# Halved inverse constants, parameters transposed on TensorE, a matmul broadcast of the log step, a pre-scaled input and a new instruction order in a state-space mixing kernel

## The chip, the cores and the metric

The kernel runs on one core of one Trainium2 chip. The metric is the device time of one execution in microseconds (us). The profile's span, from the first to the last instruction, is 1.8 us shorter than the time of the same run. "Before" and "after" below are the kernels without and with the change. Some executions fall in a second, slower state; only those in the fast state are compared.

In the traces PE is TensorE (PEld its weight loads), DVE is VectorE, ACT ScalarE, POOL GpSimd and SP SyncE; "PE ps L743" is what line 743 of the kernel writes to PSUM, the memory that holds TensorE's results, and AR is the on-chip memory SBUF. To evict is to copy a result out of PSUM. A clock, where one is shown, is TensorE's as the throttle granted it, as a share of full speed.

## The reference, cut to what matters

```python
x = A_u                                              # 2048 x 512, bf16
g = sigmoid((x * gate_w).sum(-1, keepdims=True))     # one number per row
# branch a: state-space layer, as a long convolution per channel
dt = exp(log_dt);  logdA = dt * (A_re + 1j*A_im);  dB = dt * (B_re + 1j*B_im)
P = exp(logdA[:, :, None] * arange(2048))            # 512 x 128 x 2048
K = einsum("dn,dnl,dn->dl", C_re + 1j*C_im, P, dB).real
a = irfft(rfft(pad(x)) * rfft(pad(K)))[:2048] + x * Dskip
# branch b: the two rows of x with the highest x @ w_r go through a small gated
# network; their results are added to those two rows of x
b = x + scatter(...)
return g * a + (1 - g) * b
```

The kernel computes K from two tables (powers of a step, in two levels) whose product is a matmul. The Fourier transforms are matmuls with constant matrices: the forward constants ("c_fwd") and the inverse constants ("c_inv", 2 MB). The 512 channels go in two halves, called half 0 and half 1. Branch b's updated input is written to a copy in main memory ("xp", by a scatter of two rows) and reloaded.

## The kernel before

Every operation is put on record with what it reads, what it writes and an estimated cost. A list of numbers, SEQ, then fixes the order in which all of them go to their engines; where an operation may run on ScalarE or VectorE, a minus sign means VectorE. Each engine runs its share of the list strictly in order.

```python
for n in SEQ:                                   # the fixed order
    o = ops[n if n >= 0 else ~n]
    if o.alt is not None:
        o.eng = DVE if n < 0 else ACT           # minus: VectorE
```

Cuts are marked "..." in all code below. The head: the six parameter matrices come through transposing transfers, and the log step is spread over 128 partitions by its transfer.

```python
def prm_t(i):
    P.op(SP, lambda h: h.dma_start_transpose(PRM(0, 128, i * D, (1, D)), dr(prm[i], ...)), ...)
DQ([(LDT(0, 128, 0, (1, D)), dr(A_log_dt, 0, (0, 128), (1, D)))], [], [LDT], 131072, eng=ACT)
...
AC(f512(DTB), f512(LDT), ACTF.Exp, [LDT], [DTB], tset=0)
TT(f512(AL), f512(DTB), f512(PRM, 0), ALU.mult, ...)          # the first product
```

The second table of each half is completed by two complex products, six VectorE operations each:

```python
cmul(h, sl(13, 8), sl(0, 8), bn(1, 8), ...)     # four products, a subtraction, an addition: 2048 elements each
cmul(h, sl(9, 4),  sl(5, 4), bn(0, 4), ...)     # the same with 1024
```

The forward transform is eight jobs of matmuls, each into a pair of PSUM banks that ScalarE or VectorE then evicts; there are two such pairs (`pb = fwp[k % 2]`). The spectra are multiplied on VectorE; some products are summed by accumulating transfers that the GpSimd queue issues (`dma_start(..., accum_op=add)`). The inverse constants come as one 2 MB load, behind the complex products. In the inverse, 32 matmuls subtract the input, so that g * (y - x) + x gives the result:

```python
last = hh.matmul(pb(...), G(...), X(...), start=(q + e + c == 0), stop=False)
if q:
    last = hh.matmul(pb(...), CB(0, 128, 768, (1, 128)), U(...), start=False, ...)   # minus x
```

## Time and profile before

| | before |
|---|---|
| time, median of 4 runs | 184.59 us (182.49 to 187.02) |
| profiled run, its span | 182.6 us, 180.8 us |
| VectorE busy, idle | 153.9, 26.9 us |
| first product of VectorE starts | 6.68 us |
| last product ends, last result computed, span ends | 170.0, 176.0, 180.8 us |

Those four runs spread by 4.5 us. In the five later sets of runs, of seven each, this kernel's median was 182.6 to 183.2 us. Here are lines of the DMA table (columns: output and input, issuing queue, count, size of one, median us from issue to landing):

```profile
AR<-AR POOLq DMA_DIRECT2D x8, 512.0 KB, 5.6
AR<-c_inv SPq DMA_DIRECT2D x1, 2048.0 KB, 11.5
AR<-xp SPq DMA_DIRECT2D x2, 1024.0 KB, 12.1
```

The first line is the accumulations. The second and third transfers, 4 MB together, are issued at 122.24 and 129.55 us, among those accumulations.

### The profile page before, as it was taken

The numbers are of one execution on the slowest core, as the hardware profiler recorded it, in microseconds if no ns is written. First come the engines' busy times: TensorE is split into PE (matmuls) and PEld (weight loads), VectorE is DVE, ScalarE is ACT, GpSimd is POOL, SyncE is SP. The second block draws the span as 40 slices with busy tenths as digits, with TensorE's granted clock in tenths as the row PEclk, the third lists the DMA queues.
The fourth block names the chain that finished last, engine by engine and source line by source line (L and its number), as shares of the span: only waits on it lengthen the run. The fifth ranks groups of instructions, "written<-read, shape, count | busy, mean of one in ns | idle before, by whom it ended". The sixth has DMA issues, their size and how long they took to land.

```text
span 180.8 us, 3701 instructions
## 1 busy us (share of the span) xinstructions
PE 137.5 (76%) x1550; PEld 92.1 (51%) x1558; DVE 153.9 (85%) x240; ACT 118.6 (66%) x207; POOL 18.7 (10%) x26
## 2 busy tenths in 40 slices
PE   0039797996988999759946773689739999999970
PEld 0014263432555443444614552686528788888860
DVE  0377999899999998997879999989948999999570
ACT  2599999989999799999985272163501584425100
POOL 3000000000000000001000000053100125350500
PEclk9999996999996999987997999569987999999997
DMA  5999999595703950001621000079999659979995
GB/s 56 280 325 230 284 283 381 242 450 154 266 4 99 373 170 0 4 4 15 261 67 52 0 0 5 2 141 268 305 224 356 182 100 187 163 82 186 152 186 155
DMA packets 28338, 30.25 MB, mean 167 GB/s; under 512 B 13431, under 2 KB 22914, under 8 KB 28162
## 3 DMA queue, kind: packets, MB, share of 16 engines
q1 hardware_dynamic: 22626, 23.88, 42.6%
q0 software_dynamic: 4352, 5.77, 20.1%
q10 hardware_dynamic: 1344, 0.36, 1.8%
q8 instruction: 12, 0.20, 0.4%
q14 instruction: 4, 0.03, 0.1%
HBM read 19.26 MB, written 4.20 MB: 130 GB/s over the span
## 4 chain that ended last, share of the span: by engine, by line
ACT 33%; DVE 27%; PE 24%; DMA 10%; issue 3%; DVEq 0%; ACTq 0%
DVE AR L401 26%; ACT AR L413 14%; PE ps L892 10%; DMA AR<-AR 6%; ACT AR L587 6%; PE ps L743 5%; ACT AR L417 4%; PE ps L758 4%; DMA AR<-in_A_A_re_dram 3%; ACT AR L421 3%; ACT AR L583 2%; PE ps L761 2%; PE ps L895 1%; ACT L413 1%; PE ps L805 1%
## 5 line engine op out<-in xcount | busy, mean ns | idle before, releaser
L401 DVE TENSOR_TENSOR AR<-AR 128x1024 bf16<-128x1024 bf16 (+8 forms) x135 | 120.3, 931 | 13.8 <-DMA AR<-in_A_A_re_dram 6.7
L417 ACT ACTIVATE AR<-ps 128x1024 bf16<-128x1024 f32 (+3 forms) x41 | 34.2, 856 | 31.3 <-PE ps L827 20.1
L413 ACT ACTIVATE AR<-AR 128x256 bf16<-128x256 f32 (+5 forms) x91 | 40.4, 516 | 2.9 <-DVE AR L401 1.9
L743 PE MATMUL ps<-AR 128*128 128x512 bf16 x124 | 31.7, 410 | 13.2 <-DMA AR<-in_A_u_dram 11.8
L892 PE MATMUL ps<-AR 128*128 128x256 bf16 x256 | 33.9, 279 | 3.7 <-DMA AR<-c_inv 3.3
L892 PEld LDWEIGHTS ps<-AR 128*128 128x128 bf16 x256 | 25.3, 100 | 8.1 <-DVE AR L401 4.5
L743 PEld LDWEIGHTS ps<-AR 128*128 128x128 bf16 x128 | 13.1, 105 | 29.2 <-DMA AR<-in_A_u_dram 11.8
L827 PE MATMUL ps<-AR 128*128 128x256 bf16 x160 | 21.1, 291 | 6.9 <-ACT AR L417 6.9
L827 PEld LDWEIGHTS ps<-AR 128*128 128x128 bf16 x160 | 16.3, 105 | 11.5 <-ACT AR L417 8.6
L427 POOL DMA_DIRECT2D AR<-AR x14 | 14.8, 1194 | 68.0 <-DVE AR L401 56.9
L758 PE MATMUL ps<-AR 128*128 128x512 bf16 x60 | 16.3, 412 | 3.3 <-DVE AR L417 1.3
L791 PE MATMUL ps<-AR 128*64 128x42 bf16 x512 | 11.6, 203 | 7.4 <-DVE AR L401 4.6
L413 ACT ACTIVATE AR<-ps,AR 128x256 bf16<-128x256 f32 x24 | 10.1, 473 | 10.1 <-PE ps L895 7.7
L791 PEld LDWEIGHTS ps<-AR 128*64 128x64 bf16 x512 | 11.0, 132 | 9.2 <-DVE AR L401 4.9
L587 ACT ACTIVATE AR<-AR 128x1024 bf16<-128x1024 int16 (+1 forms) x14 | 14.5, 1052 | 0.6 <-DVE AR L401 0.3
L421 DVE TENSOR_SCALAR AR<-AR 128x256 int32<-128x256 f32 (+2 forms) x42 | 12.3, 333 | 0.9 <-ACT AR L587 0.9
L758 PEld LDWEIGHTS ps<-AR 128*128 128x128 bf16 x64 | 6.4, 105 | 10.5 <-issue 2.2
L417 DVE CAST AR<-ps 128x1024 bf16<-128x1024 f32 (+2 forms) x9 | 8.7, 979 | 1.7 <-PE ps L805 0.7
L945 POOL MEMSET AR<- 128x256 bf16 x2 | 0.7, 390 | 82.2 <-PE ps L791 82.2
L895 PE MATMUL ps<-AR 128*128 128x256 bf16 x32 | 8.7, 273 | 0.0
L421 ACT ACTIVATE AR<-AR 128x256 int32<-128x256 f32 x22 | 7.9, 407 | 0.2
L583 DVE TENSOR_SCALAR AR<-AR 128x1024 int32<-128x1024 int32 (+1 forms) x9 | 6.1, 673 | 2.1 <-ACT AR L413 2.1
(50 smaller groups left out, 85.6 us busy)
## 6 DMA issues: line engine op xcount, KB each, us to landing
AR<-AR POOLq DMA_DIRECT2D x8, 512.0 KB, 5.6
AR<-c_ksp SPq DMA_DIRECT2D x5, 512.0 KB, 3.9
AR<-c_fwd SPq DMA_DIRECT2D x4, 512.0 KB, 5.8
AR<-in_A_u_dram SPq DMA_DIRECT2D x2, 1024.0 KB, 8.1
AR<-c_inv SPq DMA_DIRECT2D x1, 2048.0 KB, 11.5
AR<-xp SPq DMA_DIRECT2D x2, 1024.0 KB, 12.1
out_dram<-AR SPq DMA_DIRECT2D x16, 128.0 KB, 3.4
AR<-in_B_w_up_dram SPq DMA_DIRECT2D x2, 896.0 KB, 8.4
```

The lines of the kernel that those rows point to most:

```text
L401: return P.op(DVE, lambda h: h.tensor_tensor(out=o, in0=a, in1=b, op=op), rd, wr, cost=tt_cost(o, a, b), **k)
L413: return P.op(ACT, lambda h: h.activation(out=o, in_=a, func=func, scale=scale, bias=bias), rd, wr, cost=0.185 + nel(o) * 0.833e-3 + (0.09 ...
L417: return P.op((ACT, DVE), (lambda h: h.activation(out=o, in_=a, func=ACTF.Copy), lambda h: h.tensor_copy(o, a)), rd, wr, cost=(0.185 + n * ...
L421: return P.op((ACT, DVE), (lambda h: h.activation(out=o, in_=a, func=ACTF.Copy, scale=c), lambda h: h.tensor_scalar(out=o, in0=a, scalar1= ...
L427: P.op(POOL, lambda h: h.dma_start(o, i, accum_op=ALU.add), rd, wr, cost=1.4, nbytes=nbytes, dma=True, tag="sum")
L587: return x.activation(out=so(2), in_=lo, func=ACTF.Sin, scale=-SC16 if m else SC16, bias=HPI(0, 128, 0, (1, 1)) if m else 0.0)
L743: last = h.matmul(o, F[ft](0, 128, ((par * 4 + st) * 2 + part) * 128, (1, 128)), U(0, 128, (blk * 8 + st * 2 + par) * D, (1, D)), start=(i ...
L758: last = h.matmul(o, F[ft](0, 128, ((4 + st) * 2 + part) * 128, (1, 128)), UN(0, 128, st * D, (1, D)), start=False, stop=(st == 3 and blk ...
L791: last = hh.matmul(pb(64 * ct, 64, (g - b0) * 42, (1, 42)), TP[h][1 - part](0, 128, g * 128 + ct, (2, 64)), TQ[h][1 - part](0, 128, g * 84 ...
L827: last = hh.matmul(pb(0, 128, n * 256, (1, 256)), KPU[u](0, 128, tau * 128, (1, 128)), KC[h](0, 128, jg * 256, (1, 256)), start=(k == 0), ...
L892: last = hh.matmul(pb(0, 128, e * 256, (1, 256)), G(0, 128, ((par * 2 + part) * 4 + ft) * 512 + (2 * t2 + e) * 128, (1, 128)), X(0, 128, h ...
L895: last = hh.matmul(pb(0, 128, e * 256, (1, HC)), CB(0, 128, 768, (1, 128)), U(0, 128, (blk * 8 + (2 * t2 + e) * 2 + par) * D + h * HC, (1, ...
```

## The change

The intent is to take the known waits away and to relieve the engine that is busiest. The core of the diff, part by part, with most arguments cut:

```diff
 # 1 the head: plain loads, transposes on TensorE, a 1 KB log step spread by a matmul
-    P.op(SP, lambda h: h.dma_start_transpose(PRM(...), dr(prm[i], 0, (128, D), (1, 128))), ...)
+    DQ([(PRM(0, 128, i * D, (1, D)), dr(prm[i], 0, (D, 128), (1, D)))], [], [(PRM, i)], 131072)
+P.op(PE, lambda h: h.matmul(LP(...), ONE(0, 1, 0, (1, 128)), LDT(0, 1, 0, (1, D)), ...), ...)
+AC(f512(DTB), f512(LP), ACTF.Exp, [LP.buf], [DTB], tset=0)
+    ... last = h.transpose(pt(...), PRM(...), CB(0, 128, 0, (1, 128)))           # 24 of them
+TT(w512(AL), w512(DTB), t512(PT0), ALU.mult, [DTB, (PT0.buf, 0)], [AL])
 # 2 half 0's second table: four products, no add and no subtract; TensorE sums them
+    TT(sl(1, j, c), sl(1, s, c), bv(br), MUL, ...);  TT(sl(0, j, c), sl(0, s, c), bv(br), MUL, ...)
+    TT(xv(1), sl(0, s, c), bv(nb), MUL, ...);        TT(xv(0), sl(1, s, c), bv(bi), MUL, ...)
+    if h == 0:
+        last = hh.matmul(pb(...), TP[h][1 - part](...), EX[h][1 - part](...24 columns...), start=False, ...)
 # 3 a third PSUM pair in the forward transform (and two more banks for the table product)
-    pb = fwp[k % 2]
+    pb = (*fwp, fw2)[k % 3]
 # 4 inverse constants: two buffers of 1 MB, each with a home of its own, loaded apart
-DMA([(G(0, 128, 0, (1024, 8), (1, 1024)), dr(g_c, ...))], [], [G], 2097152)
+ld_g(0)      # right after half 1's second table in program order
+ld_g(1)      # after half 0's complex products
 # 5 the reload earlier; the input scaled by 1 - g there, and no subtraction in the inverse
+for tb in range(16):
+    P.op((ACT, DVE), (... h.activation(out=o, in_=o, func=ACTF.Copy, scale=SG(0, 128, 48 + tb, (1, 1))) ...))
-    last = hh.matmul(pb(...), CB(0, 128, 768, (1, 128)), U(...), start=False, ...)
 # 6 a new SEQ of 645 operations for 620; half of the last outputs leave on ScalarE's queue
```

## The prediction

> **What bounds the kernel now.** I read the page first (busy times, slices, chain), then the waits, then the timeline of VectorE, ScalarE and the DMA issues, and last a table by stage. The page:
>
> ```profile
> PE 137.5 (76%) x1550; PEld 92.1 (51%) x1558; DVE 153.9 (85%) x240; ACT 118.6 (66%) x207; POOL 18.7 (10%) x26
> ...
> DVE  0377999899999998997879999989948999999570
> ACT  2599999989999799999985272163501584425100
> ...
> DMA  5999999595703950001621000079999659979995
> ...
> ACT 33%; DVE 27%; PE 24%; DMA 10%; issue 3%; DVEq 0%; ACTq 0%
> ```
>
> VectorE is busy for 153.9 of 180.8 us. ScalarE is just as full in the first half (slices 2 to 21) and half idle after it. So there are two regimes: until about 95 us both engines are saturated and hand work to each other; after that VectorE alone sets the pace, and PE takes over at the very end. A gain must either take work from VectorE or close its 26.9 us of idle. The table by stage (stretch, length, then busy us and count of PE, PEld, DVE, ACT, POOL, then clock, DMA share, GB/s) says where that idle is:
>
> ```profile
> 0.00:6.68 6.68, 0.00 (x0) 0.00 (x0) 0.00 (x1) 1.91 (x2) 1.72 (x9) 1.00 0.72 101
> 6.68:15.00 8.32, 3.18 (x8) 1.19 (x9) 5.42 (x15) 7.57 (x19) 0.00 (x0) 1.00 1.07 315
> 15.00:80.00 65.00, 56.60 (x630) 29.41 (x633) 62.85 (x113) 62.65 (x115) 0.00 (x0) 0.95 0.64 200
> 80.00:100.00 20.00, 14.91 (x159) 8.61 (x163) 16.89 (x28) 16.85 (x22) 0.71 (x2) 0.84 0.28 89
> 100.00:127.00 27.00, 19.03 (x378) 15.43 (x376) 25.83 (x31) 11.16 (x19) 4.22 (x4) 0.87 0.32 78
> 127.00:140.00 13.00, 9.10 (x67) 7.32 (x68) 9.88 (x12) 3.33 (x4) 0.85 (x1) 0.87 1.02 288
> 140.00:154.20 14.20, 13.76 (x124) 11.65 (x122) 14.03 (x18) 8.40 (x14) 4.97 (x6) 1.00 0.74 159
> 154.20:175.10 20.90, 20.90 (x190) 18.50 (x190) 18.14 (x27) 6.71 (x16) 6.22 (x5) 1.00 1.03 156
> 175.10:180.80 5.70, 0.01 (x1) 0.00 (x0) 0.88 (x2) 0.00 (x0) 0.00 (x0) 0.82 0.49 142
> ```
>
> Idle of VectorE by row: 6.7 head, 2.9, 2.2, 3.1, 1.2, 3.1 (127 to 140), 0.2, 2.8, 4.8 tail. Two rows have a named cause in the waits:
>
> ```profile
> DVE AR L401 <- DMA AR<-in_A_A_re_dram: 6.7, 1, 6.7
> ...
> PE ps L892 <- DMA AR<-c_inv: 3.3, 1, 3.3
> ...
> DVE AR L401 <- DMA AR<-AR: 3.0, 2, 2.5
> ```
>
> The head is the parameter that comes through a transposing DMA. At 127 to 140 us VectorE waits for an accumulating DMA of its products while the 2 MB of inverse constants (issued at 122.24) and the 2 MB reload of the input (issued at 129.55) share the DMA engines; the chain of waits holds one such accumulation for 11.73 us, against a median of 5.6 us in the table of DMA issues. At the end PE runs without a gap from 154.2 to 175.1 us and VectorE waits for it.
>
> **What the skill says.** "VectorE: DVE Perf Modes", section "The perf-mode tier table", has a bf16 two-tensor operation of 2048 elements at 1224 ns, and at one element per cycle with fp32 or PSUM operands. The trace agrees: 1219 ns for 128x2048 bf16, and 1217 ns for 128x1024 with fp32 output. So parameters read from PSUM cost nothing extra where the output is fp32 anyway. "ScalarE: Activation LUTs", section "What ACT_TABLE_LOAD costs", has 186 ns plus 0.833 ns per element for one ACTIVATE, some 93 ns for a per-partition scale, and 93 ns of overlap back to back; the trace has 618 ns for 128x512, as it would have it. "DMA: Bandwidth & Descriptors", section "Issuing engines are not separate DMA queues", says that transfers of all issuers share the same 16 engines; the stretched accumulation above agrees. "TensorE: Matmul & The Clock Gate", section "Part 4: PE-mode transpose", says that such a transpose writes PSUM and took about 275 ns in one kernel; this trace has only four fp32 ones, of 300 ns.
>
> **Part by part.**
>
> *Head.* Six transposing DMAs go, each holding the issuing queue 1.2 to 2.1 us and landing after 5 to 8 us. Plain 128 KB loads take their place; the plain 128 KB load of the log step landed in 4.1 us. The log step itself shrinks to 1 KB (other 1 KB loads: about 5 us with three issues ahead of them; as first on its queue I estimate 3.5 to 4). Then come one small matmul (0.3), the exponential after its table load, which ends at 4.1 (0.6), and the first product (0.7). I put VectorE's first product at 5.2 us instead of 6.68, and ScalarE's exponentials at 5.9 instead of 7.40: 1.5 us. ScalarE then does 35 exponentials in a row at 313 ns (5.01 us for 16 now), to about 17 us; VectorE meanwhile has angles, the C-times-B products and the first evictions, some 12 us, so most of the 2.9 us of idle in the second row goes too. The added eviction of the transposed B costs VectorE 0.7 to 1.2 us.
>
> *VectorE work.* In the second table of half 0 the two complex products lose their add and subtract: two operations of 2048 at 1219 and two of 1024 at 687 ns, 3.8 us less; a negation of 512 comes in (0.3). The order list marks operations that VectorE takes with a minus. Counting them: 8 evictions of 1024 instead of 5 (3 x 1.22 = 3.7 more), 35 angle scalings of 256 instead of 32 (0.9 more), one 512 cast less (0.7), fewer 504 casts (0.3), fewer copies in the routing (four or so at 0.17, 0.7). With the B eviction at 1.2: -3.8 + 0.3 + 3.7 + 0.9 + 1.2 - 0.7 - 0.3 - 0.7 = +0.6 us. So VectorE's total does not fall; the saved work pays for evictions taken off ScalarE.
>
> *ScalarE work.* 3 evictions less (3.0), 3 scalings less (1.2), exponentials of the second table in halves: 18 x 0.40 instead of 9 x 0.62 (+1.7), a sixteen-part scaling of the reloaded input of which 15 are here (15 x 0.62 = 9.3). The last item is in the second regime, where ScalarE is half idle. In the first regime it loses about 2.5 us. Table loads stay at six by the order list.
>
> *PE.* Added: 256 matmuls of 24 columns for half 0; 512 of the same line take 11.6 us now, so at most 5.8 us, beside work of the saturated engines, and 24 transposes in the head. Removed: the 32 matmuls that subtract the input in the inverse (their slots in the chain are 0.11 us each), of which some 21 are in the gapless stretch at the end: 21 x 0.11 = 2.3 us.
>
> *DMA.* The inverse constants come as two loads of 1 MB, the first while the second half's tables are being multiplied; the reload comes before the products. Near the accumulations only 1 MB is left. I expect them near 5.6 us, with five products of 1.22 us to cover them: the 3.1 us wait falls to 0.5 or so.
>
> *The end.* With 2.3 us less of PE work and earlier constants, PE has no backlog. After the last product there remain 32 matmuls (3.5 us) and one pair of results, against about 5.6 us from the last product (170.0) to the end of the results: 1.5 to 2 us. Half of the second half's outputs go out on ScalarE's queue: 0.4 us at most (one issue).
>
> *Sum.* Head 1.5, gap after it 1.5, saturated stage 1.5 (ScalarE sheds 2.5, VectorE gains 1.3 there), accumulation 2.5, end 1.8, small items 0.3, less 0.6 for VectorE's total: 8.5 us. From the other side: 5.2 head + 154.5 busy + idle of 4 (saturated stage), 1.2, 0.7, 0.4, then 3.9 and 4.0 after the last product makes 173.9 against 180.8, or 6.9 us. I take 7.7: the time of 184.75 becomes 177.0 us.
>
> **Rivals.** (a) *The new order stalls ScalarE on the reload.* Ten of its scalings stand in a row ahead of evictions of the spectrum and of the second table. If the scatter into the copy of the input lands late (it took 8.3 us), in-order ScalarE waits, and then VectorE. For it: the reload took 12.1 us. Against it: VectorE has some 19 us of complex products at that point (8.1 + 7.3 + 4.1), and the scatter is no longer tied to 121 us. It would give back 3 to 5 us: 180 to 182. (b) *VectorE's work is all that counts.* Its busy time is unchanged, gaps only move elsewhere, and the accumulations still wait (now on each other); then only head and end remain: 3.5 us, 181. (c) *Better than I think*: both engines full from the head on, all of the accumulation wait gone, the saturated stage shorter by 5 us: 173 to 174. Against it is that 3% of the chain is bare hand-over.
>
> **Range and chances.** Rivals (b) and (a) set the high end, (c) the low: 173.0 to 181.3. 2% faster is 181.05. Three independent gains (head, accumulation, end) make 5.8 us together and each has a named wait, so missing 3.7 us needs two of them to fail or a new stall: 0.87 faster, 0.11 the same, 0.02 slower.
>
> **What would show it.** First product at about 5.2 us; VectorE busy 153 to 156 us in total and ScalarE's share up by some 6 us; no wait of a product on an accumulation above 1 us; no inverse matmul waiting for its constants; results ending about 4 us after the last product. Wrong if a wait of ScalarE on the reload, or of PE on an eviction, of over 3 us stands in VectorE's path, or if the first product starts after 6.5 us.

## The result

| | before | after |
|---|---|---|
| time, median of 4 runs | 184.59 us (182.49 to 187.02) | 171.59 us (171.17 to 172.36) |
| span of the profiled run | 180.8 us | 169.4 us |
| VectorE busy, idle | 153.9, 26.9 us | 153.6, 15.8 us |

The ratio is 0.9336 (95% interval 0.9247 to 0.9425). Ratios here are the mean time of one kernel's fast runs over that of the other's fast runs in the same rounds, so not quite the ratio of the medians. The direction was predicted with 0.87; the time, 171.59 us, lies 1.4 us below the range of 173.0 to 181.3. The gain is 13.0 us in these medians, 12.2 us between the means of the fast runs (183.9 and 171.7) and 11.4 us between the two profiled spans. Another chip had 172.08 against 183.16 us, so 11.1 us is the better figure: the other 2 us of the 13 lie in the four runs of the kernel before. One of these was slow, and this kernel was quicker in every later set.

The page of the kernel after has the busy times, then the slices of VectorE, ScalarE and DMA, then the engines' shares of the chain that ended last:

```profile
PE 134.3 (79%) x1807; PEld 92.3 (55%) x1807; DVE 153.6 (91%) x239; ACT 124.8 (74%) x227; POOL 18.7 (11%) x26
...
DVE  0769799999989999999999999998999999999980
ACT  2899995999999999999999266964637486456000
...
DMA  4999999949109720000760298039793194899996
...
DVE 48%; ACT 32%; PE 6%; DMA 4%; issue 4%; SPq 2%; DVEq 0%
```

VectorE's busy time is the same as before to 0.3 us. All of the gain is idle time that has gone: 26.9 - 15.8 = 11.1 us, plus those 0.3. TensorE's share of the chain fell from 24% to 6% and DMA's from 10% to 4%, so that chain now runs mostly through VectorE and, in the first half, ScalarE. The table by stage says where the idle went (columns as in the prediction: stretch, length, busy us and counts of PE, PEld, DVE, ACT, POOL, granted clock, DMA share, GB/s):

```profile
0.00:5.00 5.00, 1.64 (x9) 0.87 (x9) 0.00 (x0) 1.65 (x2) 1.61 (x9) 1.00 0.53 156
5.00:15.00 10.00, 4.57 (x24) 2.68 (x25) 8.12 (x16) 9.17 (x31) 0.00 (x0) 1.00 1.13 350
15.00:80.00 65.00, 61.53 (x878) 33.90 (x876) 62.62 (x116) 62.58 (x116) 0.00 (x0) 1.00 0.58 183
80.00:100.00 20.00, 11.78 (x197) 8.71 (x196) 19.66 (x30) 15.47 (x22) 2.45 (x3) 0.83 0.47 152
100.00:127.00 27.00, 19.55 (x388) 16.02 (x389) 26.37 (x31) 17.00 (x26) 3.47 (x4) 0.87 0.66 178
127.00:140.00 13.00, 12.19 (x111) 10.51 (x109) 12.84 (x16) 8.84 (x12) 1.72 (x2) 1.00 0.54 103
140.00:150.00 10.00, 9.46 (x87) 8.12 (x86) 10.00 (x13) 6.08 (x16) 4.13 (x5) 1.00 0.69 121
150.00:160.00 10.00, 9.90 (x90) 8.47 (x88) 9.76 (x14) 3.98 (x10) 5.36 (x5) 1.00 1.18 168
160.00:169.40 9.40, 3.67 (x32) 3.04 (x32) 4.27 (x10) 0.00 (x0) 0.00 (x0) 0.93 0.96 199
```

Subtract VectorE's busy time from the length of each row, and take the prediction's table the same way:

| VectorE idle, us | before | after | gone | the prediction's sum had |
|---|---|---|---|---|
| head, to the first product | 6.7 | 5.3 | 1.3 | 1.5 |
| to 15 us | 2.9 | 1.5 | 1.4 | 1.5 |
| 15 to 100 us (both engines full in most of it) | 5.3 | 2.7 | 2.5 | 1.5 |
| 100 to 127 us | 1.2 | 0.6 | 0.5 | 0.3 (small items) |
| 127 to 140 us (accumulations) | 3.1 | 0.2 | 3.0 | 2.5 |
| 140 us to the start of the last row (175.1 and 160) | 2.9 | 0.2 | 2.7 | 1.8 |
| last row | 4.8 | 5.1 | -0.3 | 0 |
| VectorE's work | | | 0.3 | -0.6 |

The differences are taken before rounding. The row from 15 to 100 us hides a split: from 15 to 80 us VectorE's idle did not fall (2.2 and 2.4), and all of the gain is from 80 to 100 us (3.1 and 0.3). The waits of over 0.2 us that stood there before were on ScalarE (1.0, 0.9 and 0.3) and on a small matmul (0.7), none on a forward job. The two kernels reach the same point at different times, so rows of fixed times do not hold quite the same work. Fixed points of the program agree with it. From before to after, the first complex product of half 1 starts at 95.2 and 90.3 us, the first accumulation is issued at 117.3 and 111.7, the last product ends at 170.0 and 160.8, and the results end at 176.0 and 164.8: a lead of 4.9, 5.5, 9.2 and 11.2 us.

The waits of VectorE and ScalarE after (columns: us in total, times, longest):

```profile
DVE AR L403 <- ACT AR L415: 5.3, 1, 5.3
DVE AR L419 <- PE ps L550: 1.3, 1, 1.3
DVE AR L403 <- PE ps L819: 0.5, 1, 0.5
ACT AR L993 <- DMA AR<-xp: 1.4, 1, 1.4
```

The wait of 3.0 us of a product on an accumulation and the wait of 3.3 us of an inverse matmul on its constants have no successor in this list. The first line is the head: the first product now waits for ScalarE's exponential, no longer for a parameter. VectorE's timeline shows the second half (columns: start, us, instruction, count, idle before it and who ended it):

```profile
116.91 16.26 DVE L403 TENSOR_TENSOR AR<-AR 128x2048 bf16<-128x2048 bf16 x18 [0.54 <-PE ps L819]
...
133.64 27.13 DVE L403 TENSOR_TENSOR AR<-AR 128x2048 bf16<-128x2048 bf16 x34
161.31 3.50 DVE L410 SCALAR_TENSOR_TENSOR AR<-ps,AR 128x256 bf16<-128x256 f32 x8 [0.54 <-PE ps L940]
```

The 34 products run as one block to 160.77 us and the eight results follow as one block too, at 4.0 us after the last product in all. Before, results came in four pairs, each waiting for TensorE. The transfers (columns as above):

```profile
AR<-AR POOLq DMA_DIRECT2D x8, 512.0 KB, 4.8
AR<-xp SPq DMA_DIRECT2D x2, 1024.0 KB, 7.3
AR<-c_inv SPq DMA_DIRECT2D x2, 1024.0 KB, 8.5
```

The reload is issued at 94.84 us and the first half of the constants right behind it, the second half at 116.9. So 3 of the 4 MB are through before the accumulations.

### The profile page after: what moved, and what is told of

Read it like the earlier page. It is cut to its first block, busy times and chain, and to the rows that moved or that the text cites. A ratio compares the mean times of both kernels' runs of the same rounds, so it can differ in the third digit from the quotient of the medians.

```text
span 169.4 us, 4237 instructions
## 1 busy us (share of the span) xinstructions
PE 134.3 (79%) x1807; PEld 92.3 (55%) x1807; DVE 153.6 (91%) x239; ACT 124.8 (74%) x227; POOL 18.7 (11%) x26
## 3 DMA queue, kind: packets, MB, share of 16 engines
q0 software_dynamic: 4352, 5.77, 21.6%
## 4 chain that ended last, share of the span: by engine, by line
DVE 48%; ACT 32%; PE 6%; DMA 4%; issue 4%; SPq 2%; DVEq 0%
DVE AR L403 41%; ACT AR L415 14%; ACT AR L611 5%; PE ps L773 5%; DMA AR<-c_fwd 4%; ACT AR L419 4%; ACT AR L423 4%; DVE AR L419 3%; ACT AR L607 3%; SPq L426 2%; DVE AR L410 2%; DVE AR L423 2%; ACT L221 1%; ACT L415 1%; PE ps L940 1%
## 5 line engine op out<-in xcount | busy, mean ns | idle before, releaser
L403 DVE TENSOR_TENSOR AR<-AR 128x2048 bf16<-128x2048 bf16 (+6 forms) x127 | 111.9, 928 | 1.5 <-PE ps L819 0.5
L415 ACT ACTIVATE AR<-AR 128x256 bf16<-128x256 f32 (+4 forms) x99 | 40.2, 486 | 3.1 <-DVE AR L423 2.0
L940 PE MATMUL ps<-AR 128*128 128x256 bf16 x256 | 29.6, 273 | 1.7 <-DVE AR L403 1.7
L940 PEld LDWEIGHTS ps<-AR 128*128 128x128 bf16 x256 | 24.6, 98 | 5.6 <-DVE AR L403 2.8
L858 PE MATMUL ps<-AR 128*128 128x256 bf16 x160 | 19.8, 279 | 3.0 <-ACT AR L419 3.0
L773 PEld LDWEIGHTS ps<-AR 128*128 128x128 bf16 x128 | 12.7, 101 | 17.3 <-ACT AR L419 2.1
L819 PE MATMUL ps<-AR 128*64 128x42 bf16 x512 | 14.9, 197 | 5.9 <-DVE AR L403 3.5
L858 PEld LDWEIGHTS ps<-AR 128*128 128x128 bf16 x160 | 15.4, 100 | 6.4 <-ACT AR L419 4.4
L819 PEld LDWEIGHTS ps<-AR 128*64 128x64 bf16 x512 | 14.2, 123 | 7.7 <-DVE AR L403 4.2
L788 PE MATMUL ps<-AR 128*128 128x512 bf16 x64 | 15.6, 379 | 0.6 <-ACT AR L419 0.6
L423 DVE TENSOR_SCALAR AR<-AR 128x256 int32<-128x256 f32 (+3 forms) x45 | 13.2, 337 | 0.6 <-ACT AR L611 0.4
L836 PE MATMUL ps<-AR 128*32 128x128 bf16 (+1 forms) x96 | 7.3, 420 | 7.3 <-ACT AR L419 7.3
L419 DVE CAST AR<-ps 128x1024 bf16<-128x1024 f32 (+2 forms) x11 | 11.2, 1035 | 1.3 <-PE ps L773 1.3
L993 ACT ACTIVATE AR<-AR 128x512 bf16<-128x512 bf16 x15 | 9.8, 714 | 1.4 <-DMA AR<-xp 1.4
L836 PEld LDWEIGHTS ps<-AR 128*32 128x32 bf16 x96 | 4.6, 122 | 9.8 <-ACT AR L419 8.3
L788 PEld LDWEIGHTS ps<-AR 128*128 128x128 bf16 x64 | 5.8, 97 | 7.0 <-ACT AR L419 0.7
(59 smaller groups left out, 111.7 us busy)
```

The source lines that it names most:

```text
L403: return P.op(DVE, lambda h: h.tensor_tensor(out=o, in0=a, in1=b, op=op), rd, wr, cost=tt_cost(o, a, b), **k)
L415: return P.op(ACT, lambda h: h.activation(out=o, in_=a, func=func, scale=scale, bias=bias), rd, wr, cost=0.185 + nel(o) * 0.833e-3 + (0.09 ...
L419: return P.op((ACT, DVE), (lambda h: h.activation(out=o, in_=a, func=ACTF.Copy), lambda h: h.tensor_copy(o, a)), rd, wr, cost=(0.185 + n * ...
L423: return P.op((ACT, DVE), (lambda h: h.activation(out=o, in_=a, func=ACTF.Copy, scale=c), lambda h: h.tensor_scalar(out=o, in0=a, scalar1= ...
L773: last = h.matmul(o, F[ft](0, 128, ((par * 4 + st) * 2 + part) * 128, (1, 128)), U(0, 128, (blk * 8 + st * 2 + par) * D, (1, D)), start=(i ...
L788: last = h.matmul(o, F[ft](0, 128, ((4 + st) * 2 + part) * 128, (1, 128)), UN(0, 128, st * D, (1, D)), start=False, stop=(st == 3 and blk ...
```

## The experiments

Eighteen kernels ran, in five sets, each set on one chip, with three rounds and with the kernel before in it. Unless a line says so, results were correct. Two questions: which parts made the gain, and why was it larger than predicted? My theory at first was that the gain is a sum of the parts' own gains, as the prediction added them. The rival was that a single wait taken away is absorbed by the next one, and that only the whole, with an order fitted to it, pays.

### One part of the change alone, in the kernel before, its order kept

**Plain parameter loads** (the parameters then lie untransposed, so the result is wrong):

```diff
-h.dma_start_transpose(PRM(0, 128, i * D, (1, D)), dr(prm[i], 0, (128, D), (1, 128)))
+h.dma_start(PRM(0, 128, i * D, (1, D)), dr(prm[i], 0, (D, 128), (1, D)))
```

> The kernel before with its six transposing parameter loads replaced by plain 128 KB loads into the same buffers, all else as it was (values are then in the wrong places, so the result is wrong on purpose). Theory (my head step): the first product starts 1.5 to 2 us earlier and the time falls by 1.5 to 3 us, because ScalarE and VectorE are saturated right behind it. Rival (order alone): the old order was fitted to the late start, so the head gain is eaten by later waits and the time falls by less than 0.7 us.

Measured: 182.31 us, ratio 0.9982 (0.9932 to 1.0033). The head's wait fell from 6.7 to 5.3 us, and two waits of VectorE appear in the profile that were shorter or absent:

```profile
DVE AR L417 <- PE ps L743: 2.8, 2, 2.2
DVE AR L421 <- DMA AR<-in_A_u_dram: 2.3, 1, 2.3
```

VectorE starts 1.4 us earlier and then waits for TensorE's first forward jobs and for the input. Only the second wait goes clearly with the early start: the next three runs, which keep the old head, have the first one at 1.8 to 2.2 us too, and the second at 0.5 us or less. The head alone is worth nothing; the rival was right.

**One eighth of the inverse constants** (wrong):

```diff
-DMA([(G(0, 128, 0, (1024, 8), (1, 1024)), dr(g_c, ...))], ...)
+DMA([(G(0, 128, 0, (1, 1024)), dr(g_c, ...))], ...)
```

> The kernel before, loading only one eighth of the inverse constants (256 KB in place of 2 MB; the rest of that buffer holds old data, so the result is wrong on purpose). Theory (collision of transfers): the accumulating transfers of the first products land in 5 to 7 us in place of up to 11.7, the 3.0 us wait of VectorE for them goes below 1 us, and the time falls by 2 to 3 us. Rival: the 2 MB reload that runs at the same time is enough to stretch them, the wait stays above 2 us and the time falls by under 1 us.

Measured: 183.04 us, ratio 1.0006 (0.9942 to 1.0069). The wait on accumulations stays at 2.9 us, and the reload moved up to 127.26 us, into the same accumulations. The rival was right: taking most of this transfer away does not end that wait.

**One quarter of the reload** (wrong):

```diff
-dr(xp, 1024 * j * D, (2 * D, 128), (256 * D, 4), (1, 2 * D))
+dr(xp, 1024 * j * D, (2 * D, 128), (1, 2 * D))
```

> The kernel before, reloading only a quarter of the input (512 KB in place of 2 MB; wrong result on purpose), with all of its 2 MB of inverse constants. Theory (the reload, not the constants, stretches the accumulating transfers): the wait of VectorE for them falls under 1 us from 3.0, where the run with fewer constants kept 2.9. What it is worth in time: 1 to 3 us if VectorE's products set the second half, under 1 us if PE's work at the end does. Rival: either transfer alone is enough, and the wait stays above 2 us.

Measured: 182.94 us, ratio 0.9989 (0.9936 to 1.0042). The wait on accumulations is 3.4 us. So cutting either load leaves the wait as it was. How far the two loads make it is not shown: no run cut both, and with both whole the wait was 3.0 us in the kernel before, but 1.6 with plain parameter loads and 1.8 without subtracting matmuls (the next run).

**No subtracting matmuls in the inverse** (wrong): the 32 matmuls with the identity are deleted.

```diff
-if q:
-    last = hh.matmul(pb(...), CB(0, 128, 768, (1, 128)), U(...), start=False, ...)
```

> The kernel before without the 32 matmuls that subtract the input in the inverse (wrong result on purpose). Theory (PE holds the end): PE's gapless stretch at the end shortens by 21 slots of 0.11 us, VectorE's waits for it shrink, and the time falls by 1.5 to 2.3 us. Rival (VectorE's products hold the end all the same): it falls by under 0.8 us.

Measured: 180.62 us, ratio 0.9875 (0.9831 to 0.9918), so 2.3 us. That is the size that the prediction gave for TensorE's 21 slots of 0.11 us at the end. In the profile 1.7 us of it lie there: from the last product to the last result it takes 4.3 us in place of 6.0. The rest lies earlier, where the wait on accumulations, which this edit does not touch, is 1.2 us shorter.

**The first, second and fourth of these together** (wrong):

> The three edits of the other runs together in the kernel before (wrong result on purpose). If the three gains lie on one path one after the other they add up: 5.5 to 7.5 us less, about 178 us. What is then left of the 13 us belongs to the division of the work, the smaller VectorE work of half 0 and the new order. Rival: these three explain all of it (172 to 173 us), or, being partly hidden behind VectorE, they add up to under 4 us.

Measured: 181.41 us, ratio 0.9935 (0.9885 to 0.9984), less of a gain than the last one alone. The gains of single parts do not add up in the old order.

**A third PSUM pair** (two routing steps of TensorE had to move later in the order, as they share those banks):

```diff
-pb = fwp[k % 2]
+pb = fw3[k % 3]          # fw3 = [*fwp, PB("fw2", 2, None)]
```

> The kernel before with a third PSUM pair in the forward transform, its own order kept (two routing steps had to move later). Theory (the third pair pays only with an order made for it): the time changes by less than 1.5 us. Rival (the pair by itself is the gain, since taking it away from the changed kernel cost over 13 us): it falls by 4 us or more.

Measured: 188.54 us, ratio 1.0302 (1.0243 to 1.0361): 5.9 us slower, outside both expectations. Its profile has VectorE waiting 2.0, 2.0 and 1.8 us for small matmuls of branch b (L672, L708, L719), where the kernel before waited 0.4, less than 0.2 and 0.4 us. That points to the steps that had to move, so this run does not price the pair.

### One part undone in the kernel after, its order kept

**The kernel after once more**, as the yardstick of this set:

> The changed kernel itself, unedited, as the anchor for the other runs of this call. Expected: ratio to the kernel before 0.93 to 0.945, about 171 to 172 us, and the same picture: VectorE busy 153 to 154 us, idle about 16 us of which 10 to 11 lie before its first and after its last product.

Measured: 172.08 us, ratio 0.9398 (0.9330 to 0.9466).

**The complex products of half 0 whole again**, with add and subtract, and without the 256 extra matmuls:

```diff
-if h == 1:
+if True:
     cmul(h, ...)
-if h == 0:
+if False:
     last = hh.matmul(pb(...), TP[h][1 - part](...), EX[h][1 - part](...), ...)
```

> The changed kernel with the two complex products of half 0 made whole again on VectorE (four subtractions and additions back, the negation and the 256 small matmuls out; the result stays right). Theory (VectorE's work is on the path from its first to its last product, nearly without a gap): VectorE gains 3.8 us and loses 0.3, and the time rises by 3 to 3.8 us against the anchor. Rival (ScalarE sets the saturated stage, VectorE has room there): it rises by less than 1.5 us.

Measured: 175.07 us, ratio 0.9527 (0.9427 to 0.9628). One of its four runs was slow; the fast ones average 174.6 us, 2.6 us over the kernel after (172.0). VectorE's busy time rose from 153.6 to 156.9, by 3.3, and the prediction had counted 3.8 less 0.3. So in this order the part is worth most of its VectorE time.

**Three forward evictions on ScalarE in place of VectorE**, at the same places of the order (-205, -214, -223 become 204, 213, 222):

> The changed kernel with three evictions of the forward transform (those that run on VectorE at 47 to 68 us) given back to ScalarE, where the old division had them. Theory (ScalarE sets the saturated stage, as the chain of the changed kernel says): VectorE is 3.6 us shorter there but ScalarE 3.0 us longer, and the time rises by 1 to 3 us. Rival (VectorE's total is all that counts): it falls by 2 to 3.6 us.

Measured: 178.43 us, ratio 0.9736 (0.9666 to 0.9806), 6.4 us slower than the kernel after, twice what the theory allowed. VectorE has 3.1 us less work, and ScalarE 3.0 us more:

```profile
DVE AR L413 <- PE ps L749: 9.3, 1, 9.3
...
PE ps L788 <- ACT AR L415: 8.8, 1, 8.8
```

VectorE waits 9.3 us for a small TensorE result of branch b's network, and TensorE itself stands 8.8 us before a forward matmul (L788) for ScalarE. Is it ScalarE's load, or the place of an eviction in ScalarE's queue?

**One of the three on ScalarE, but ahead of the exponentials in the order**, looks at that:

```diff
-... 242 240 241 311 313 209 ... 289 278 -205 206 ...
+... 242 240 241 204 311 313 209 ... 289 278 206 ...
```

> The changed kernel with one forward eviction (at 47.7 us on VectorE) given to ScalarE, but put ahead of the long run of exponentials in ScalarE's queue, not into it. Theory (what cost 6 us in the run with three such evictions was their place behind 39 exponentials, holding a PSUM pair, not ScalarE's load): ratio 0.93 to 0.945, as the changed kernel. Rival (ScalarE's load in the saturated stage): 1 us or more slower than the changed kernel, ratio above 0.946.

Measured: 171.60 us, ratio 0.9410 (0.9348 to 0.9471), the same as the kernel after. One eviction more on ScalarE (1.0 us) costs nothing if it stands early in the queue, so the load of one is not what costs. That all three would be free there, or that one in its old place would cost, was not tried.

**Two evictions and one scaling at 112 to 116 us on ScalarE** (-385, -452, -462 become 384, 451, 461), where ScalarE is half idle:

> The changed kernel with two evictions and one scaling in its second half (at 112 to 116 us) moved from VectorE to ScalarE, which is idle for a third of that time. Theory (VectorE alone sets the second half): VectorE has 2.2 us less and the time falls by 1 to 2.2 us, ratio to the kernel before 0.928 to 0.935. Rival (the hand-over through PSUM makes the wait longer than the work saved): no change, or up to 1 us more.

Measured: 171.76 us, ratio 0.9392 (0.9342 to 0.9441), no change. VectorE's busy time fell by 2.0 us, and one wait of its products on TensorE's table product grew from 0.5 to 3.8 us. That product stood 2.4 us for ScalarE, which now had three evictions of the table product in a row to do. So the rival was right: the hand-over through PSUM took back what VectorE had saved.

**A head that is late on purpose**: a table load of 1.28 us before the first exponential.

```diff
-AC(f512(DTB), f512(LP), ACTF.Exp, [LP.buf], [DTB], tset=0)
+P.op(ACT, lambda h: (h.preload_act_table_set("silu_and_others"), h.activation(out=f512(DTB), in_=f512(LP), func=ACTF.Exp))[1], ...)
```

> The changed kernel with one useless activation table load of 1.28 us ahead of the first exponential, so that its first product starts about 1.3 us later, at 6.6 us. Theory (in the changed kernel nearly every microsecond between first and last product is VectorE's or ScalarE's work, so the head counts in full): the time rises by 1.0 to 1.5 us against the changed kernel, ratio to the kernel before 0.944 to 0.949. Rival (the head is absorbed here too, as it was in the kernel before): it rises by less than 0.5 us.

Measured: 171.59 us, ratio 0.9394 (0.9349 to 0.9439), no change. The first product waits 6.6 us in place of 5.3, and the waits behind it (on TensorE's transposes and on its first forward job) shrink from 1.3 and 1.3 us to 0.2 and 0.5. So the 1.3 us that the head gained are worth nothing in this kernel either. The first forward matmuls, 8 us of them, start at 12.3 us in the kernel after, once their constants have landed, and at 12.1 us here: the late head does not move them.

**Two PSUM pairs again** (ten positions of the order had to move later to stay free of deadlock):

```diff
-pb = (*fwp, fw2)[k % 3]
+pb = fwp[k % 2]
```

> The changed kernel with two PSUM pairs in the forward transform in place of three (ten issue positions have to move later so that the order stays possible). Theory (the third pair is what lets the early start be used: with two pairs the evictions wait for PE, as the kernel before with plain parameter loads showed 2.2 and 1.4 us of such waits): the time rises by 1.5 to 4 us, with waits of evictions for the forward matmuls of over 2 us in VectorE's path. Rival (only the order matters): it rises by less than 0.8 us.

Measured: 187.31 us, ratio 1.0185 (1.0092 to 1.0278): about 15 us slower than the kernel after (14.6 between the means of the fast runs), far beyond both expectations. The profiled execution fell in the slow state, so only its waits are read; the largest is this one:

```profile
DVE AR L704 <- PE ps L709: 7.2, 2, 6.3
```

L709 is a step of the routing, not a forward job; VectorE's evictions waited 9.9 us in total for forward matmuls. Of the parts undone here this one costs the most. But this is not yet what the pair is worth, since an order made for three pairs stalls with two.

### Orders fitted to each structure

The order list and the engine choices were searched again, with the same effort for each kernel, by a simulated search over the kernel's own list of costs. Only the times measured on the chip are claims here.

**The kernel before, only SEQ changed:**

> The kernel before with nothing changed but its order list (and the choice of engine for the operations that may run on either): a new list, searched for on the kernel's own list of costs with the longer transfer waits that the change also put there. Theory (the order carries most of the gain): ratio 0.95 to 0.97, about 175 to 178 us, which is half to two thirds of what the change brought. Rival (the structure carries it: fewer products, third PSUM pair, halves of the constants): ratio above 0.985.

Measured: 178.13 us, ratio 0.9726 (0.9664 to 0.9788), just short of the theory. One of its runs fell in the slow state; the fast ones average 177.7 us. The accumulation wait is not gone, it doubled:

```profile
DVE AR L401 <- DMA AR<-AR: 6.0, 4, 2.5
```

**The kernel after, only SEQ changed:**

> The changed kernel with only its order list replaced by one from the same search with the same effort (result stays right). Theory (the order is still loose): 163 to 168 us, ratio 0.89 to 0.92, better than both kernels. Rival (the changed kernel is at the floor that VectorE's 153.6 us of work sets with head and tail): no better than 0.935.

Measured: 168.29 us, ratio 0.9181 (0.9114 to 0.9247). It is correct and beats both kernels. No product waits for an accumulation. One run of it fell in the slow state as well; the fast ones average 167.7 us, and those of the kernel before in this set 182.7. So a better order by itself is worth 182.7 - 177.7 = 5.0 us to the old structure, and with fitted orders the new structure is 177.7 - 167.7 = 10.0 us ahead of the old one.

**Two PSUM pairs with an order fitted to them:**

> The changed kernel with two PSUM pairs in the forward transform (the edit that cost 15 us with the order kept) and an order searched for that case. Theory (the pair has no worth of its own, only the order fitted to it): within 1.5% of the re-ordered changed kernel of this call. Rival (the pair itself is worth several us): over 2.5% slower than that one.

Measured: 171.19 us, ratio 0.9363 (0.9310 to 0.9417), and its mean of 171.1 us is 3.3 us (2.0%) over the fast runs of the re-fitted kernel after: between what the theory (1.5%) and the rival (2.5%) allowed. So of the 15 us with the order kept, at least 11 were misfit. That the other 3.3 are the pair's is not shown. The profile has nothing of them in the forward transform: the row from 15 to 80 us (columns as in the tables by stage) leaves VectorE 0.3 us of idle, less than the 2.1 of the re-fitted kernel with three pairs. What is longer is the wait before the first product, 7.7 us against 5.2, and a wait on accumulations that the three-pair kernel does not have:

```profile
15.00:80.00 65.00, 62.16 (x954) 34.24 (x953) 64.75 (x121) 64.03 (x134) 0.00 (x0) 0.97 0.53 181
...
DVE AR L403 <- PE ps L550: 7.7, 1, 7.7
...
DVE AR L403 <- DMA AR<-AR: 2.3, 2, 1.2
```

So the difference may as well be the luck of one search.

**Both halves of the inverse constants late, order fitted:**

```diff
-ld_g(0)
 ...
+ld_g(0)      # next to ld_g(1), and each reads KC[1], so that it waits for half 1's evictions
 ld_g(1)
```

> The changed kernel with both halves of the inverse constants held back until the second table's values are evicted (so neither goes out right behind the first complex products), and with the order searched again with the same effort as for the re-fitted changed kernel (ratio 0.9181 to before, 168.3 us). Theory (an early first half in a home of its own is worth something in its own right): the ratio is at least 0.015 higher, 0.933 or more, and products wait on accumulating transfers again for 3 to 6 us, as they do in the re-fitted kernel before. Rival (with an order fitted to it, the place of the constants does not matter): within 0.01 of 0.918, and no such wait above 1 us.

Measured: 172.85 us, ratio 0.9486 (0.9414 to 0.9557), in the mean 5.2 us over the fast runs of the re-fitted kernel (another set, on another chip; the ratios differ by 0.0305, or 5.6 us). The theory's number held, its mechanism did not: no product waits for an accumulation. The constants are issued at 115.71 us, and TensorE's timeline and VectorE's waits show another chain:

```profile
124.79 1.89 PE L940 MATMUL ps<-AR 128*128 128x256 bf16 x8 [4.95 <-DMA AR<-c_inv]
```

```profile
DVE AR L403 <- PE ps L868: 3.5, 1, 3.5
DVE AR L410 <- PE ps L940: 2.4, 1, 2.4
```

In-order TensorE stands 4.95 us before its first inverse matmul. A small matmul that VectorE's next product needs comes behind it in the same queue, so VectorE waits 3.5 us; and TensorE's backlog at the end shows as 2.4 us before the results, against 0.5. VectorE's idle is 3.2 us above the re-fitted kernel's (22.8 against 19.6), and the span is 3.5 us longer.

**The complex products of half 0 whole, order fitted:**

> The changed kernel with the two complex products of half 0 whole again, as in the run with whole products, but with the order searched again with the same effort. Theory (the four two-input operations that they add cost VectorE time that no order hides): 2 to 3.5 us over the re-fitted changed kernel, so a ratio of 0.929 to 0.937, and VectorE's busy time 2 to 4 us above that kernel's 147.3. Rival (most of the 3.0 us measured in the kept order was misfit of the order): within 0.01 of 0.918.

Measured: 176.82 us, ratio 0.9685 (0.9625 to 0.9745), so 9.0 us over the fast runs of the re-fitted kernel and even 1.6% in ratio above the same structure in the kept order. VectorE's busy time rose by only 2.2 us (149.5 against 147.3). The rest is laid here to bad luck of the search, and the trace shows where it may lie. The first line below is GpSimd's timeline, with the scatter of two rows into the copy of the input; the second is VectorE's at that time:

```profile
94.43 13.77 POOL L757 DMA_INDIRECT xp<-AR  x1 [11.15 <-DVE AR L407]
```

```profile
94.02 12.77 DVE L403 TENSOR_TENSOR AR<-AR 128x2048 bf16<-128x2048 bf16 x14
```

The scatter takes 13.77 us, from the start of a block of 14 products until just after its end; in the kernel after it took 1.72 us, beside single operations. The reload waits for it, is issued at 109.64 us with all of the inverse constants behind it, and these land 17.6 and 21.6 us after their issue, among the accumulations. Products then wait 5.8 us for accumulations and ScalarE waits 8.7 us for the reload.

Why the scatter takes so long stays open. The Trainium skill, "SBUF — State Buffer", section "SBUF: two separate sides", has VectorE and GpSimd share a pair of ports as an exclusive lock: a VectorE operation with two inputs in SBUF shuts out a GpSimd operation that reads SBUF, for the whole instruction. The scatter takes its row numbers from SBUF, so that fits this trace. But in the re-fitted kernel before, VectorE did such products without a gap all through the scatter, and it took only this long:

```profile
121.46 1.68 POOL L727 DMA_INDIRECT xp<-AR  x1 [0.31 <-issue]
```

In the two re-fitted kernels with three pairs it took 3.9 (constants late) and 4.5 us, the former ending in the middle of a block of products. No run here tests the cause. As a price of the complex products this run is worthless, then; the 2.6 us in the kept order are the only ones. It also says that a searched order can be off by several us, since the list of costs that it is searched with has no such stall. The 10.0 us above carry that uncertainty, and so do the 3.3 us of the pair and the 5.2 us of the late constants: each structure was searched once.

## Why the prediction was right or wrong

**The direction and most of the signs to look for were right.** VectorE's busy time is unchanged (153.6; predicted 153 to 156), its gaps closed, and the lists of waits lost the two named waits. ScalarE's share rose by 6.2 us (predicted about 6). The first product started at 5.34 us (5.2), and results ended 4.0 us after the last product (about 4). Before, that stretch took 6.0 us (170.0 to 176.0), not "about 5.6" as the prediction read it. Scaling the reloaded rows took 714 ns, not 620: with its per-partition scale, which is near the 706 ns (186 + 512 x 0.833 + 93) that can be estimated from the figures in the Trainium skill, "ScalarE: Activation LUTs", section "What ACT_TABLE_LOAD costs"; the prediction had cited it and not applied its last term.

**The second sum failed.** "From the other side: 5.2 head + 154.5 busy + ... then 3.9 and 4.0 after the last product makes 173.9" counts the eight results twice: they take 8 x 0.44 = 3.5 us, they are part of the 154.5 us of busy time, and they fill nearly all of the 3.9 us after the last product. Without the double count that sum is 170.4 us, and the measured span is 169.4. "I take 7.7" averaged a sum of 8.5 with one that had an error of 3.5 us in it.

**The first sum failed by the size of four terms.** It has 8.5 us, and the rows of the table above give 11.4. "Saturated stage 1.5" measured 2.5, "accumulation 2.5" 3.0, "end 1.8" 2.4 (the last two rows of idle together), and "less 0.6 for VectorE's total" was a gain of 0.3; the others are within 0.2 us. In VectorE's total, the two-input products of 2048 and 1024 elements took 5.0 us less, where the prediction had 3.8. In the saturated stage it priced ScalarE's and VectorE's work only and has no term for the third PSUM pair, though that is in the diff. But the idle that went there lay after 80 us, mostly in waits for ScalarE, and two pairs with a fitted order leave less idle in the forward stage than three (0.3 us against 2.1). So what the runs show is a hand-over to ScalarE that shrank by more than predicted; which part of the change did it stays open.

**Two terms had the right size for the wrong reason.** "Head 1.5, gap after it 1.5": VectorE's idle there did fall by 1.3 and 1.4 us, but plain loads in the kernel before and a late head in the kernel after both left the time unchanged. The head isn't an independent gain; when it came earlier the waits behind it grew, and when it came later they shrank by as much. And "Near the accumulations only 1 MB is left. I expect them near 5.6 us": that row's idle did vanish (3.0 us, predicted 2.5) and the accumulations took 4.8. But a load of an eighth of the constants, or a quarter of the reload, leaves that wait standing in the old order, and the run with late constants has none of it. What takes the wait away is not shown. What the early constants bring, in the one run that takes them back, is TensorE's earlier start of the inverse: 3.5 us between the spans and 5.2 between the fast runs, in fitted orders.

**"Three independent gains" is therefore the step that misled the range.** The rows of idle are not independent prices: one by one, in an order made for another structure, the parts measured 0, 0, 0, -2.3 and +5.9 us (the last with two other steps moved). Rivals (a) and (b) did not come to pass (ScalarE waited 1.4 us on the reload; the waits did not move elsewhere), and (c), which had 173 to 174, was the nearest and still too slow. What the runs attribute: subtracting matmuls 2.3 us (old order), complex products 2.6 (new order kept) and early constants 3.5 to 5.2 (fitted orders). These come to 8.4 to 10.1 us, or 11.7 to 13.4 with the 3.3 us that are not shown to be the third pair's. That is near the 11.1 but isn't a decomposition of it, as they are taken in three different orders. The early reload and the scaled input by themselves stay unpriced.

**And the starting point was high.** 184.75 us was the median of three runs, one of them slow, and the profile that every step used was of a 182.6 us run. Later sets had 182.6 to 183.2. The same 7.7 us from 182.8 would have been 175.1, still 3.5 too slow.

## What to carry to other kernels

In a kernel with a fixed order on in-order engines, price a change with an order fitted to it and compare it with the old structure in an order searched with the same effort, and more than once: one search here was off by several us. A single part tried in an order made for something else can read 0 or even the wrong sign. When you add up a time from stages, let each instruction stand in one term only, and give every hunk of the diff a term, even if it is "0, because". A wait on a transfer that runs beside two large ones need not shrink when one of these does; cut both before you name the cause.

## What the Trainium skill lacked or had wrong

- "SBUF — State Buffer", section "SBUF: two separate sides": its timed case of a stalled transfer is a plain one beside a copy; it has no figure for a scatter beside two-input products. Here a scatter of two rows took 13.77 us beside 14 of them in a row (12.77 us), 1.72 us beside single operations, and 1.68 us in another kernel beside products without a gap. So the lock held for one instruction does not by itself tell how long a scatter takes. No run tests the cause.
- Nothing that the prediction cited was contradicted: a bf16 product of 2048 elements took 1218 ns, the per-partition scaling 714 ns, and a transpose in the head 314 ns (median of 24) where the prediction had cited some 275.
